# Batch 0 of an attention and gated FFN kernel, by blocks of 128 queries for all heads

## The chip, the core and the metric

The kernel runs on one core of a Trainium2 chip. The metric is the device time of one execution in microseconds (us); lower is better. A core has five engines that run side by side, each through its own queue in order: TensorE (PE in the profile, its weight loads PEld), VectorE (DVE), ScalarE (ACT), GpSimd (POOL) and SyncE (SP). They wait for each other by semaphores. Matrix products go into PSUM, a small memory that TensorE writes and ScalarE and VectorE read; all other tiles lie in SBUF.

## The reference

Eight batches of 576 queries and keys, eight heads of 64 columns, 16 extra "beacon" keys that every query sees:

```python
k_all = np.concatenate([beacon_k, k], axis=2)          # (8, 8, 16 + 576, 64)
v_all = np.concatenate([beacon_v, v], axis=2)
scores = q @ k_all.T / 8                               # causal on the 576, beacons always seen
a = softmax(scores)
x = (a @ v_all).transpose(0, 2, 1, 3).reshape(4608, 512)
g = x @ w_gate                                         # 512 -> 1536
out = (g * sigmoid(g) * (x @ w_val)) @ w_out           # 1536 -> 512
```

Inputs and output are float32; the kernel multiplies in bfloat16.

## The kernel before

**Data.** Queries and keys of batches 0 to 2 are loaded with 64 x 9 rows a head: partition p holds rows 9p to 9p + 8 (or, of a part of them, a shorter run). TensorE turns them (`turn`, tile `t_ps`) so that head columns lie on partitions, and VectorE or ScalarE copies them to `qT` and `kT` (`turned_copy`). Later batches are turned by DMA. GpSimd issues nearly all loads, since its transfers convert float32 to bfloat16 on the way; they go through one queue in order (`order_of_loads`). Only the first keys and queries of batch 0 (256 rows of heads 0 to 3, tile `first`) come by SyncE's and ScalarE's queues in float32, and are converted by VectorE and ScalarE (`regroup`, `regroup_second`); so are the beacon keys of batch 0 (`first_beacons`, converted by `cast_beacons`).

**Attention.** Two heads make a pair; a batch has four. Scores are made transposed (keys on partitions, queries along the row) in units. A unit is up to 512 columns of one pair, filled by a few matmuls into one tile `s_ps` (`scores`); ScalarE turns it into `p` by one exponential (`exponent`). `UNITS` lists the units of a pair: "A" has the first 240 queries (`HEAD`), "B", "C" and "D" the other 336 in wide pieces. The causal triangle is cut either on TensorE (a masked unit adds `below`) or afterwards by VectorE with `upper` or by GpSimd (`mask`). Value products take `p` as stationary operand (`pv`, tile `pv_ps`), one column more giving the sum of weights; `normalize` divides and writes `x`, tokens on partitions. Of batch 0, queries 0 to 239 go ahead: `pv_front`, `normalize_front`, `x_turn_front` and `x_copy_front` make the first 240 columns of `xT`, so that six gate tiles of 240 tokens can run before the rest is there; `x_turn` and `x_copy` then bring columns 240 to 575, a pair at a time.

**FFN.** `xT` is cut into nine chunks of 512 tokens. A gate tile (`ffn`, `gate_value`, tile `gv_ps`) makes 128 of the 1536 gate columns and the same value columns for one chunk, in two halves (G and H). ScalarE makes a tanh of the gate half (`tanh`), VectorE two products (`act1`, `act2`, tile `hT`). `project` multiplies by `wo`, `evacuate` copies and stores. In chunk 0 gate columns f = 0 to 5 come in two tiles each: 240 tokens (`HEAD`), then 272.

**Order.** PSUM has four slots; each of `t_ps`, `s_ps`, `pv_ps`, `gv_ps` and so on takes one (`take`), and it comes back when its last reader is done (`give`), first come, first served. The order of all work is written out by hand in the string `plan`: each letter is one piece (S and s scores, plain and masked; E exponential; D and M mask; P and p value products; Z, N, J, I the front's value products, normalizing, turn and copy; G, H gate halves; a, 1, 2 tanh and the two products; T turn; K, k, Q, q copies of turned keys and queries by VectorE and ScalarE; l a load; h a warming matmul pair; F a projection step). An engine runs its pieces in the order of the string. `warm` and `keep_warm` issue matmuls whose results nobody reads.

Of the kernel before, what the change touches and what calls it, by code (L numbers as in the profile page):

```python
# [33 lines left out]
FRONT = 4  # L34
# [35 lines left out]
FIRST_UNITS = "A0 A1 A2 A3 B0 C0 D0 B1 C1 D1 B2 C2 D2 B3 C3 D3"  # L70


HEAD = 240


def p_col(t, q):
    if t == 0:
        return q if q < HEAD else 368 + q - HEAD
    if t == 1:
        return 240 + q - 112 if q < HEAD else 784 + q - HEAD  # L80
    if t == 3:
        return 1120 + q - 368 if q < 496 else 1584 + q - 496
    return 1248 + q - HEAD if t == 2 else 704 + q - 496


@with_exitstack
def kernel(
# [88 lines left out]
    def keep_warm(ps):  # L176

        while heat:
            heat.pop()
            for row in range(2):  # L180
                r = slice(HALF * row, HALF * row + HALF)
                nc.tensor.matmul(ps[:, row, 0:P], lhsT=ident[r, :], rhs=ident[r, :], start=True, stop=True)  # L182
# [9 lines left out]
    first_beacons = static.tile([NB, H * D], FP32, name="first_beacons")  # L192
# [7 lines left out]
    p_first = static.tile([P, 2, 368], BF16, name="p_first")  # L200
# [73 lines left out]
    def cast_beacons():  # L274
        nc.vector.tensor_copy(beacons[0][0:NB, :], first_beacons[:])

# [9 lines left out]
    def turn(n):  # L286
# [3 lines left out]
        key = ("t", n)  # L290
        t_ps = turned[n] = take(key, [P, 2, 1024], BF16, "t_ps")
        parts[n] = 2 * len(pairs)
        side = sides.pop(n - NFT, None)
        for j, m in enumerate(pairs):
            by_head = qk[b % 2][:, 2 * RUN * m : 2 * RUN * (m + 1)].rearrange("p (h i d) -> p h i d", i=ROWS, h=2)
            for i in range(w):
                cols = slice(HALF * (w * j + i), HALF * (w * j + i + 1))
                for hh in range(2) if side is None else (None,):
                    for row in range(2):
# [3 lines left out]
                        halves(key, row, row, t_ps[o, row, cols], of, ident[r, r], 1, 1, True)  # L303
        if n >= NFT and 0 in pairs:
            beacon_turn(b, key, t_ps)
# [4 lines left out]
    def beacon_turn(b, key, t_ps):  # L310
# [14 lines left out]

    def first_beacon_turn():
        key = ("t", "beacons")
        t_ps = turned["beacons"] = take(key, [P, 2, 1024], BF16, "t_ps")
        beacon_turn(0, key, t_ps)

    def first_beacon_copy(eng):
        beacon_copy(0, turned["beacons"], eng)
        give(("t", "beacons"))

    def turned_copy(c, is_k, eng):
# [36 lines left out]
    def p_of(b, m, first):  # L372
        return p_first if b == 0 and m == NPAIR - 1 and first else pt[(NPAIR * b + m) % NPT]
# [32 lines left out]
    def exponent(n):  # L406
# [3 lines left out]
        nc.scalar.activation(p_of(b, m, u == "A")[:, :, c0 : c0 + w], ps[:, :, 0:w], ACT.Exp, scale=0.125)  # L410
# [21 lines left out]
    def pv_front(n):  # L432

        o_ps = fronts[n] = take(("z", n), [P, 2, 512], FP32, "pvf_ps")
        keep_warm(o_ps)
        for m in (2 * n, 2 * n + 1):
            for hh in range(2):
                for c in range(2):
                    for t in range(c + 1):
                        col = p_col(t, QBLOCKS[c][0])  # L440
                        at = 136 * (m % 2) + 68 * c
                        nc.tensor.matmul(
                            o_ps[:, hh, at : at + D + 1],
                            lhsT=p_of(0, m, True)[:, hh, col : col + P],
# [435 lines left out]
```

## Time and profile before

| | |
|---|---|
| median of 3 runs | 366.99 us (365.69 to 368.39) |
| the profiled execution | 366.46 us |
| its span, first to last instruction | 364.6 us |
| mean granted TensorE clock | 0.993 |
| TensorE busy | 353.5 us, 97% of the span |
| VectorE, ScalarE, GpSimd busy | 224.8, 186.0, 123.2 us |
| moved by DMA | 39.88 MB |

The durations come from one profiled execution. A row of a timeline gives start, length, engine, line, operation, output and inputs, how many instructions are merged, and in brackets how long the engine had been idle and what released it. A matmul's end is modelled, so its length holds some time in which the next already runs.

### The profile page before, as it was taken

Reading aid. Unit: us, or ns where it says so; the run is one execution under the profiler, and the core shown is the slowest. Engines: PE = TensorE matmul, PEld = TensorE weight load, DVE = VectorE, ACT = ScalarE, POOL = GpSimd, SP = SyncE. Lnnn points to the kernel's source line nnn. Section 1 sums busy time; section 2 is a strip of 40 time slices with the busy share of each in tenths; the row PEclk is TensorE's granted clock in tenths of the full one; section 3 lists DMA queues with packets and bytes.
Section 4 is the critical chain, followed back from the end, with each engine's and each line's share of the span. In section 5 each row is a group of like instructions: output and inputs, shape, how many; then the busy total and the mean of one; then the engine's idle time right before and its main releaser. Section 6 shows DMA issues by size and latency. Waiting matters only on the chain.

```text
span 364.6 us, 11957 instructions
## 1 busy us (share of the span) xinstructions
PE 353.5 (97%) x5202; PEld 200.8 (55%) x5202; DVE 224.8 (62%) x433; ACT 186.0 (51%) x280; POOL 123.2 (34%) x186
## 2 busy tenths in 40 slices
PE   5899999999999999999999999999999999999994
PEld 3678565654444565554565566546655554455543
DVE  5858986567766664487428753775567765364451
ACT  2875899822424777544863576457633323222310
POOL 8935677836237545365433013012000000000000
PEclk9899999999999999999999999999999999999999
DMA  9999999999999999999989829621413000110113
GB/s 150 155 199 194 189 192 135 179 133 181 178 131 111 135 134 126 150 178 137 120 138 139 106 39 112 105 15 21 110 59 67 0 2 3 58 59 2 59 59 117
DMA packets 146133, 39.88 MB, mean 109 GB/s; under 512 B 131488, under 2 KB 141728, under 8 KB 146080
## 3 DMA queue, kind: packets, MB, share of 16 engines
q0 software_dynamic: 97136, 18.87, 70.2%
q1 hardware_dynamic: 48512, 19.92, 28.9%
q8 instruction: 41, 0.67, 0.8%
q10 hardware_dynamic: 432, 0.33, 0.3%
q14 instruction: 12, 0.10, 0.1%
HBM read 38.27 MB, written 9.44 MB: 131 GB/s over the span
## 4 chain that ended last, share of the span: by engine, by line
PE 92%; ACT 4%; DMA 1%; DVE 1%; SPq 0%; issue 0%; DVEq 0%
PE gv_ps L168 51%; PE o_ps L168 25%; PE s_ps L168 6%; PE pv_ps L168 4%; PE pv_ps L498 4%; ACT p L410 3%; DMA first<-in_k_dram 1%; PE t_ps L166 1%; ACT kT L256 0%; PE xt_ps L541 0%; DVE hT L596 0%; DVE u L589 0%; SPq L661 0%; PE s_ps L182 0%; SPq L654 0%
## 5 line engine op out<-in xcount | busy, mean ns | idle before, releaser
L168 PE MATMUL gv_ps<-xT,wv 64*128 64x512 bf16 (+2 forms) x912 | 203.5, 365 | 0.0
L168 PE MATMUL gv_ps<-xT,wg 64*128 64x512 bf16 (+2 forms) x912 | 203.1, 365 | 0.1
L584 ACT ACTIVATE th<-gv_ps 128x512 f32<-128x512 f32 (+2 forms) x114 | 65.4, 575 | 117.9 <-PE gv_ps L168 117.6
L410 ACT ACTIVATE p<-s_ps 128x832 bf16<-128x832 f32 (+2 forms) x127 | 104.5, 873 | 32.6 <-PE s_ps L168 29.3
L168 PE MATMUL o_ps<-wo,hT 64*128 64x512 bf16 (+2 forms) x912 | 116.8, 365 | 0.2
L589 DVE SCALAR_TENSOR_TENSOR u<-th,gv_ps 128x512 f32<-128x512 f32 (+2 forms) x114 | 74.7, 656 | 65.1 <-ACT th L584 64.5
L168 PEld LDWEIGHTS <-wg 64*128 64x128 bf16 x912 | 82.3, 94 | 46.1 <-PE gv_ps L168 2.7
L168 PEld LDWEIGHTS <-wv 64*128 64x128 bf16 x912 | 81.6, 94 | 39.8 <-issue 0.7
L596 DVE SCALAR_TENSOR_TENSOR hT<-gv_ps,u 128x512 bf16<-128x512 f32 (+2 forms) x114 | 74.6, 661 | 3.0
L168 PEld LDWEIGHTS <-hT 64*128 64x128 bf16 x912 | 42.6, 94 | 33.5 <-PE o_ps L168 1.2
L219 POOL DMA_DIRECT2D vb<-in_v_dram x40 | 33.9, 850 | 66.5 <-PE s_ps L168 28.9
L168 PE MATMUL s_ps<-qT,kT 64*128 64x336 bf16 (+3 forms) x512 | 42.6, 253 | 1.6 <-ACT p L410 1.0
L168 PEld LDWEIGHTS <-kT 64*128 64x128 bf16 x512 | 24.2, 95 | 21.7 <-issue 1.1
L219 POOL DMA_DIRECT2D qk<-in_q_dram x25 | 21.3, 852 | 24.1 <-DMA qT<-qk 6.3
L527 DVE TENSOR_TENSOR x<-pv_ps,rec 128x640 bf16<-128x640 f32 (+1 forms) x32 | 25.3, 791 | 1.2
L419 DVE TENSOR_TENSOR p<-p,upper 128x256 bf16<-128x256 bf16 (+2 forms) x70 | 19.8, 308 | 9.5 <-ACT p L410 9.3
L526 DVE RECIPROCAL rec<-pv_ps 128x10 f32<-128x10 f32 (+1 forms) x32 | 6.8, 213 | 29.2 <-PE pv_ps L168 22.9
L219 POOL DMA_DIRECT2D qk<-in_k_dram x25 | 21.3, 855 | 8.2 <-PE gv_ps L168 4.7
L258 DVE COPY o_sb<-o_ps 128x512 f32<-128x512 f32 (+2 forms) x20 | 12.6, 653 | 18.1 <-PE o_ps L168 15.1
L423 POOL TENSOR_SCALAR_AFFINE_SELECT p<-p 128x256 bf16<-128x256 bf16 (+2 forms) x47 | 18.1, 404 | 14.9 <-ACT p L410 14.5
L168 PEld LDWEIGHTS <-p 64*128 64x128 bf16 x960 | 18.8, 94 | 4.5 <-PE pv_ps L168 0.2
L168 PE MATMUL pv_ps<-vb,p 64*128 64x65 bf16 x960 | 19.9, 189 | 0.0
(67 smaller groups left out, 144.6 us busy)
## 6 DMA issues: line engine op xcount, KB each, us to landing
out_dram<-o_sb SPq DMA_DIRECT2D x34, 256.0 KB, 2.7
vb<-in_v_dram POOLq DMA_DIRECT2D x24, 128.0 KB, 5.7
qk<-in_q_dram POOLq DMA_DIRECT2D x21, 128.0 KB, 5.3
qk<-in_k_dram POOLq DMA_DIRECT2D x16, 128.0 KB, 5.0
wo<-in_moe_w_out_dram POOLq DMA_DIRECT2D x2, 768.0 KB, 13.2
wg<-in_moe_w_gate_dram POOLq DMA_DIRECT2D x3, 384.0 KB, 10.9
wv<-in_moe_w_val_dram POOLq DMA_DIRECT2D x3, 384.0 KB, 12.6
qk<-in_k_dram POOLq DMA_DIRECT2D x2, 576.0 KB, 10.0
```

What stands on the lines that cost most here:

```text
L168: ins = nc.tensor.matmul(o, lhsT=l, rhs=r, start=start, stop=stop)
L219: return nc.gpsimd.dma_start(dst[p0 : p0 + n, c, :, 0:D], src[b, :, r : r + n, :].rearrange("h j d -> j h d"))
L258: eng.tensor_copy(o, i)
L410: nc.scalar.activation(p_of(b, m, u == "A")[:, :, c0 : c0 + w], ps[:, :, 0:w], ACT.Exp, scale=0.125)
L419: nc.vector.tensor_tensor(out=ap, in0=ap, in1=upper[:, None, d : d + w].to_broadcast([P, 2, w]), op=ALU.mult)
L423: nc.gpsimd.affine_select(out=ap, in_=ap, compare_op=ALU.is_ge, fill=0.0, base=d, pattern=[[0, 2], [1, w]], channel_multiplier=-1,)
L498: ins = nc.tensor.matmul(o_ps[:, side, 68 * c : 68 * c + D + 1], lhsT=pt[n % NPT][:, side, col : col + P], rhs=vb[b % 2][:, t, 2 * m + sid ...
L526: nc.vector.reciprocal(rec[:, :, c0:NKT], o[:, :, :, D : D + 1])
L527: nc.vector.tensor_tensor(out=xs[b][:, c0:NKT, P * m : P * m + P].rearrange("p c (h d) -> p h c d", d=D), in0=o[:, :, :, 0:D], in1=rec[:, ...
L584: nc.scalar.activation(th[:, 0:w], gvs[n][:, 0, 0:w], ACT.Tanh, scale=0.5)
L589: nc.vector.scalar_tensor_tensor(out=u[:, 0:w], in0=ths[n][:, 0:w], scalar=1.0, in1=gvs[n][:, 0, 0:w], op0=ALU.add, op1=ALU.mult)
L596: nc.vector.scalar_tensor_tensor(out=hTs[j][:, f, c0:c1], in0=gvs.pop(n)[:, 1, 0 : c1 - c0], scalar=0.5, in1=ths.pop(n)[:, 0 : c1 - c0], o ...
```

## The change

Batch 0 no longer goes in a front of 240 queries and a rest by pairs. It goes by query blocks: the first 240 queries, then 128, 128 and 80, and in each block all four pairs are done before the next. The parts:

- The turns of batch 0 are cut at 256 and at 384 rows (`FRONT`, `MIDDLE`), and so are its loads: K0m and Q0m bring rows 256 to 383 of all heads, K0t and Q0t the rest.
- Pairs 0 and 1 get a PSUM slot each for keys and for queries (`APART`) in their first turn. The beacon keys are turned into the slot of the first keys.
- The beacon keys of batch 0 are loaded by GpSimd as its first transfer, already converted; SyncE's transfer and VectorE's `cast_beacons` go.
- Score units "2", "3", "4" replace "B", "C", "D" in batch 0. Their matmuls are 128 or 80 columns wide, 112 matmuls instead of 64, with the same sum of columns.
- `pv_front` to `x_copy_front` now serve all blocks, so `pv`, `normalize`, `x_turn` and `x_copy` of batch 0 go.
- `p` of the fourth pair lies in a borrowed `hT` buffer (`lent`), since four pairs are open at a time.
- Chunk 0's gate tiles for f = 0 to 5: three of 240 tokens, three of 128, three of 368 and six of 144, fifteen instead of twelve.
- The plan is a new one up to the start of batch 1, and loads stand in a new order up to those of batch 2. The rest of the plan is the same.

The core of the diff:

```diff
-TURNS = [
-    (0, (0,), 0, FRONT), (0, (1,), 0, FRONT), (0, (2, 3), 0, FRONT), (0, (0, 1), FRONT, ROWS), (0, (2, 3), FRONT, ROWS)
-]
+FRONT, MIDDLE = 4, 6
+TURNS = [(0, (0,), 0, FRONT), (0, (1,), 0, FRONT), (0, (2, 3), 0, FRONT)]
+TURNS += [(0, m, i0, i1) for i0, i1 in ((FRONT, MIDDLE), (MIDDLE, ROWS)) for m in ((0, 1), (2, 3))]
+APART = 2
...
-FIRST_UNITS = "A0 A1 A2 A3 B0 C0 D0 B1 C1 D1 B2 C2 D2 B3 C3 D3"
-HEAD = 240
+UNITS["2"] = (368, 384, [(t, 128 * t, 240, 128) for t in range(3)], [(256, P, 0)])
+UNITS["3"] = (752, 512, [(t, 128 * t, 368, 128) for t in range(4)], [(384, P, 0)])
+UNITS["4"] = (1264, 400, [(t, 80 * t, 496, 80) for t in range(5)], [(320, 80, 0)])
+HEAD, BODY = 240, 368
...
-    p_first = static.tile([P, 2, 368], BF16, name="p_first")
+    lent = hT_pool.tile([P, NF, TOK], BF16, name="hT", tag="hT")
+    p_lent = lent[:].rearrange("p f t -> p (f t)")[:, 0 : 2 * P_W].rearrange("p (h w) -> p h w", h=2)
...
-        key = ("t", n)
-        t_ps = turned[n] = take(key, [P, 2, 1024], BF16, "t_ps")
-        parts[n] = 2 * len(pairs)
+        keys = [("t", n, 0), ("t", n, n < APART)]
+        for key in keys[: 1 + (n < APART)]:
+            turned[key] = take(key, [P, 2, 1024], BF16, "t_ps")
+            parts[key] = len(pairs) if n < APART else 2 * len(pairs)
+        parts[keys[0]] += n == 0
...
         if n < 16:
-            u, m = FIRST_UNITS.split()[n]
-            return 0, int(m), u
+            return 0, n % 4, "A234"[n // 4]
...
-    def x_turn_front(n):
-        if n == 0:
-            fronts["x"] = take("xf", [P, 2, 1024], BF16, "xf_ps")
+    def x_turn_front(n):
+        key = "xf" if n < 2 else ("xf", n)
+        if n != 1:
+            fronts[key] = take(key, [P, 2, 1024], BF16, "xf_ps")
...
-    ffn = [(0, f, c0, c1) for c0, c1 in ((0, HEAD), (HEAD, TOK)) for f in range(NF // 2)]
+    ffn = [(0, f, c0, c1) for c0, c1 in ((0, HEAD), (HEAD, BODY)) for f in range(NF // 4)]
+    ffn += [(0, f, 0, BODY) for f in range(NF // 4, NF // 2)] + [(0, f, BODY, TOK) for f in range(NF // 2)]
...
-    nc.sync.dma_start(
-        first_beacons[:].rearrange("j (h d) -> j h d", d=D), beacon_k[0].rearrange("h j d -> j h d")
-    )
...
     nc.scalar.activation(pt[1][:, 0, 0:1], pt[2][:, 0, 0:1], ACT.Exp)
+    beacon_load(0)
     runs(0, k, 4, H, 0, FRONT)
     runs(0, q, 4, H, 0, FRONT)
...
-    warm(8, TOK)
-    warm(4, P)
+    warm(7, TOK)
+    warm(6, P)
...
-    K0.0 Q0.0 v0.2 v0.1 v0.0 Q0.4 K0.4 v0.3 v0.4 v0.5 g0 u0 u1 g1 g2 u2 b1 K1 Q1 u3 g3 v1.2 v1.4 u4 g4 v1.0 K2 b2
+    K0m Q0m v0.2 v0.1 v0.0 K0t Q0t g0 u0 g1 u1 v0.3 v0.4 g2 u2 v0.5 b1 Q1 b2 K1 u3 g3 u4 v1.0 g4 Q2 K2 v1.3 v1.4
...
-    lb0h9ThlWQlAKhUTThllhqKlQhSlBsETKKQlEsSEEDQSlkZSlEDNEZsDlEJisTlhNEsDQhEJKhsllsslEEPIlElpSPsREllE
+    h0hTlWq9lTlhkAlSlTEhhlhlhBhhhqlqKKSElUlThsTsEEKKQDSllDsEElZlQSEZNJThNklqISDJlITlEsDGQKsEHSEDESa1
...
```

What this does to the engines' queues shows at three places. First GpSimd, from the fourth of its loads on; `upper` and `below` are the masks, `vb` values, `wg` and `wv` gate and value weights. Before:

```order
L209 DMA qk_101<-in_q_dram 64x4x320
L219 DMA vb_103<-in_v_dram 128x8x64
L685 AFFINE_SELECT upper<-upper 128x144
L219 DMA vb_103<-in_v_dram 112x8x64
L219 DMA vb_103<-in_beacon_v_dram 16x8x64
L209 DMA qk_101<-in_q_dram 64x4x320
L209 DMA qk_101<-in_k_dram 64x4x320
L679 AFFINE_SELECT below<-below 64x256 x2
```

After the change, from the same value load on:

```order
L226 DMA vb_102<-in_v_dram 128x8x64
L226 DMA vb_102<-in_v_dram 112x8x64
L226 DMA vb_102<-in_beacon_v_dram 16x8x64
L216 DMA qk_100<-in_k_dram 64x8x192
L216 DMA qk_100<-in_q_dram 64x8x192
L696 AFFINE_SELECT below<-below 64x256 x2
L255 DMA wg<-in_moe_w_gate_dram 128x4x128
L255 DMA wv<-in_moe_w_val_dram 128x4x128
L702 AFFINE_SELECT upper<-upper 128x144
```

`upper` moved from behind the first value load to behind the first two weight loads, and it now follows `below`.

Second ScalarE at its start, from its conversion of the first rows on (`p_109` to `p_111`, later `p_108` to `p_110`, are the three `p` buffers). Before:

```order
L256 ACTIVATE qk_101<-first 128x256
L256 ACTIVATE qT_105<-t_ps 128x256
L410 ACTIVATE p_109<-s_ps 128x2x368
L410 ACTIVATE p_110<-s_ps 128x2x368
L410 ACTIVATE p_111<-s_ps 128x2x368
L410 ACTIVATE p_first<-s_ps 128x736
L256 ACTIVATE kT_107<-t_ps 128x320
```

After:

```order
L263 ACTIVATE qk_100<-first 128x256
L263 ACTIVATE qT_104<-t_ps 128x256
L263 ACTIVATE kT_106<-t_ps 128x256
L418 ACTIVATE p_108<-s_ps 128x2x368
L263 ACTIVATE qT_104<-t_ps 128x256
L263 ACTIVATE qT_104<-t_ps 128x2x256
L418 ACTIVATE p_109<-s_ps 128x2x368
L418 ACTIVATE p_110<-s_ps 128x2x368
L418 ACTIVATE hT<-s_ps 128x2x368
```

Three more copies of turned rows are ScalarE's, two of them between the first exponential and the second.

Third ScalarE again, around the first tanh (`th`). Before:

```order
L410 ACTIVATE p_109<-s_ps 128x2x416
L410 ACTIVATE p_109<-s_ps 128x2x464
L584 ACTIVATE th<-gv_ps 128x240
L410 ACTIVATE p_109<-s_ps 128x2x416
L584 ACTIVATE th<-gv_ps 128x240
L256 ACTIVATE xT<-xt_ps 128x336 x2
```

After:

```order
L418 ACTIVATE p_110<-s_ps 128x2x512
L603 ACTIVATE th<-gv_ps 128x240
L418 ACTIVATE hT<-s_ps 128x2x512
L603 ACTIVATE th<-gv_ps 128x240
L418 ACTIVATE p_108<-s_ps 128x2x400
L418 ACTIVATE p_109<-s_ps 128x2x400
L263 ACTIVATE xT<-xf_ps 128x4x128
L603 ACTIVATE th<-gv_ps 128x240
L418 ACTIVATE p_110<-s_ps 128x2x400
L603 ACTIVATE th<-gv_ps 128x128
```

Before, one exponential of batch 0 was left at the first tanh; now five are, and tanh and exponentials alternate.

More of the change, by code (lines that the diff above doesn't have):

```diff
@@ L181, in keep_warm @@
                 r = slice(HALF * row, HALF * row + HALF)
-                nc.tensor.matmul(ps[:, row, 0:P], lhsT=ident[r, :], rhs=ident[r, :], start=True, stop=True)
+                nc.tensor.matmul(ps[:, row, at : at + P], lhsT=ident[r, :], rhs=ident[r, :], start=True, stop=True)
     ident = static.tile([P, P], BF16, name="ident")
@@ L302, in turn, with beacon_turn @@
                         of = side[r, i] if hh is None else by_head[r, hh, i0 + i]
-                        halves(key, row, row, t_ps[o, row, cols], of, ident[r, r], 1, 1, True)
+                        halves(keys[row], row, row, turned[keys[row]][o, row, cols], of, ident[r, r], 1, 1, True)
         if n >= NFT and 0 in pairs:
-            beacon_turn(b, key, t_ps)
+            beacon_turn(b, keys[0])
     BEACONS_AT = S
     parts = {}
-    def beacon_turn(b, key, t_ps):
+    def beacon_turn(b, key):
+        t_ps = turned[key]
         for mm in range(NPAIR):
@@ L324, in beacon_copy, with copied @@
         )
+    def copied(key, k):
+        parts[key] -= k
+        if not parts[key]:
+            give(key)
     def first_beacon_turn():
-        key = ("t", "beacons")
-        t_ps = turned["beacons"] = take(key, [P, 2, 1024], BF16, "t_ps")
-        beacon_turn(0, key, t_ps)
+        beacon_turn(0, ("t", 0, 0))
     def first_beacon_copy(eng):
-        beacon_copy(0, turned["beacons"], eng)
-        give(("t", "beacons"))
+        beacon_copy(0, turned["t", 0, 0], eng)
+        copied(("t", 0, 0), 1)
     def turned_copy(c, is_k, eng):
@@ L367, in unit, with p_of @@
         if n < 16:
-            u, m = FIRST_UNITS.split()[n]
-            return 0, int(m), u
+            return 0, n % 4, "A234"[n // 4]
         return n // 16, n % 16 // 4, "ABCD"[n % 4]
-    def p_of(b, m, first):
-        return p_first if b == 0 and m == NPAIR - 1 and first else pt[(NPAIR * b + m) % NPT]
+    def p_of(b, m):
+        return p_lent if b == 0 and m == NPAIR - 1 else pt[(NPAIR * b + m) % NPT]
     def scores(n, masked):
@@ L495, in pv @@
             for c, (q0, _) in enumerate(QBLOCKS):
-                for t in range(c + 1) if b or c > 1 else ():
+                for t in range(c + 1):
                     col = p_col(t, q0)
@@ L533, in normalize @@
         give(("p", n))
-    xts = {}
-    def x_turn(m):
-        t_ps = xts[m] = take(("x", m), [P, 2, 1024], BF16, "xt_ps")
-        for c, (q0, n) in enumerate(QBLOCKS):
-            if q0 >= HEAD:
-                nc.tensor.transpose(t_ps[:, 0, q0 : q0 + n], xs[0][0:n, c, P * m : P * m + P], ident[0:n, 0:n])
-    def x_copy(m, eng):
-        copy(eng, xT[:, m, HEAD:S], xts.pop(m)[:, 0, HEAD:S])
-        give(("x", m))
     def x_transpose(b):
@@ L837 @@
+    FaHFaFF1FFF12FHa2FG1GFHF2HFaF1FoaFFoFFFFFG2FF1FFHFaF1FGFF2HGFFFaFF12FH2FFaFFFFF1FFFFF2oFFFFFFFFF
+    FFFOFFFFFFOFFFFOFFFOFFFFOFFFFFFFFOo
     """
```

179 lines of the change are left out of this document (94 added, 85 removed).

## The prediction

> **What bounds the kernel now.** I read the page first, then busy time by stretch, then the timelines of the first 37 us, and last the chain that ended last.
>
> ```profile
> PE 353.5 (97%) x5202; PEld 200.8 (55%) x5202; DVE 224.8 (62%) x433; ACT 186.0 (51%) x280; POOL 123.2 (34%) x186
> ```
>
> TensorE is busy for 97% of the span, so only about 11 us are open at all. The view by stretch says where they lie (columns: busy us of PE, PEld, DVE, ACT, POOL with instruction counts, then PE's granted clock, DMA share, GB/s):
>
> ```profile
> 0.00:4.82 4.82, 3.29 (x8) 1.16 (x9) 2.64 (x16) 1.91 (x3) 3.62 (x10) 1.00 0.58 123
> 4.82:8.22 3.40, 1.19 (x49) 0.78 (x51) 1.58 (x4) 0.00 (x0) 3.40 (x7) 1.00 1.47 187
> 8.22:11.64 3.42, 3.42 (x132) 2.96 (x120) 2.73 (x8) 1.84 (x3) 3.35 (x6) 0.51 1.75 167
> 11.64:15.05 3.41, 2.69 (x48) 1.90 (x45) 2.91 (x12) 3.40 (x6) 3.41 (x5) 0.99 1.96 142
> 21.45:26.93 5.48, 5.42 (x117) 4.38 (x115) 3.48 (x10) 3.71 (x8) 1.77 (x3) 1.00 1.26 204
> 26.93:37.03 10.10, 9.88 (x193) 8.03 (x192) 8.24 (x21) 5.87 (x16) 5.44 (x7) 1.00 1.49 197
> 72.00:364.60 292.60, 287.62 (x3888) 155.00 (x3884) 172.50 (x306) 132.35 (x196) 70.95 (x107) 1.00 0.87 94
> ```
>
> Behind 21.45 TensorE hardly stops, and the change rewrites only batch 0 and the first gate tiles. So its worth is decided in the first 37 us: TensorE stands still for 2.2 us between 4.82 and 8.22, and then runs a stretch of 3.4 us at half clock. From 11.64 on ScalarE has no gap (3.40 of 3.41), and TensorE waits for its exponentials. The chain starts like this (start, us, what):
>
> ```profile
> 1.61 0.83 SPq L661
> 2.50 4.95 DMA first<-in_k_dram
> 7.55 0.44 DVE qk L258
> 8.03 0.71 PE t_ps L166 x48
> ```
>
> The beacon keys' transfer (L661) stands on SyncE ahead of the second pair's keys, and these open the first transposes. My yardstick is the first gate tile that is 512 wide (f = 6). It starts at 37.03 before; in both kernels batch 0, half the first chunk and a little of batch 1 lie ahead of it. Before the change 18 transposes fewer and two score units more are done there, 0.25 us each way, so the two starts can be compared.
>
> ```profile
> 6.77 0.32 PE L166 MATMUL t_ps<-ident,qk 64*64 64x64 bf16 x16 [1.49 <-DVE qk L258]
> 9.29 0.82 PE L168 MATMUL s_ps<-qT,kT 64*128 64x240 bf16 x8
> 12.49 0.52 PE L442 MATMUL pvf_ps<-vb,p 128*128 128x65 bf16 x12
> 21.45 0.27 PE L168 MATMUL gv_ps<-xT,wg 64*128 64x240 bf16 x1
> 37.03 0.38 PE L168 MATMUL gv_ps<-xT,wg 64*128 64x512 bf16 x1
> ```
>
> These are before's milestones: first transposes, first scores, first value products, first gate tile, yardstick. I work out the same five for the changed kernel, following each engine's queue and each PSUM slot.
>
> **1. The start, beacon keys and keys of pair 1.**
>
> ```profile
> 5.81 0.71 DVE L275 CAST beacons<-first_beacons 16x512 bf16<-16x512 f32 x1 [1.72 <-DMA first_beacons<-in_beacon_k_dram]
> 7.55 0.43 DVE L258 CAST qk<-first 128x512 bf16<-128x512 f32 x1 [0.83 <-DMA first<-in_k_dram]
> 4.35 0.42 ACT L256 ACTIVATE qk<-first 128x256 bf16<-128x256 f32 x1 [0.63 <-DMA first<-in_k_dram]
> ```
>
> The first keys are there at 4.35, when ScalarE casts its half. VectorE's half stood behind the beacon cast until 6.45; that cast goes, so both halves are done at 4.77, and the transposes start when the warming matmuls end, at about 5.1 instead of 6.77. The keys of pair 1 move from SyncE's third place to its second, from 2.50 to 1.61. Their transit lies between that of the first keys (0.81 to 4.35, 3.5 us) and the 4.95 us of the chain: landing at 5.1 to 6.6, taken as 5.9. Cast, turn 1, beacon copy and six warming matmuls follow: first scores at **6.85, 2.4 us earlier**. The beacon keys, first on GpSimd, need at most the same 4.2 us as on SyncE (1.61 to 5.81) from 1.33, so 5.5; they are wanted at 6.3.
>
> **2. ScalarE up to the fourth exponential.**
>
> ```profile
> 8.40 0.39 ACT L256 ACTIVATE qT<-t_ps 128x256 bf16<-128x256 bf16 x1 [3.63 <-PE t_ps L166]
> 11.65 0.78 ACT L410 ACTIVATE p<-s_ps 128x736 bf16<-128x736 f32 x1 [0.35 <-PE s_ps L168]
> 12.33 0.78 ACT L410 ACTIVATE p_first<-s_ps 128x736 bf16<-128x736 f32 x1
> 13.31 2.48 ACT L410 ACTIVATE p<-s_ps 128x832 bf16<-128x832 f32 x3
> 15.63 0.63 ACT L256 ACTIVATE xT<-xf_ps 128x480 bf16<-128x480 bf16 x1
> ```
>
> Two exponentials of 736 columns start 0.68 apart though each shows 0.78: back to back they overlap by 0.1. Exponential 0 runs 7.4 to 8.15. Then two copies of queries, now ScalarE's, hold it until 9.0 (0.39 and about 0.64, less the overlap), and scores 1 come behind 14 warming matmuls. Exponentials 1 to 3 end at 11.4, against 13.11 (12.33 + 0.78): **1.7 us earlier**, 0.7 of the lead being spent.
>
> **3. GpSimd, the mask and the first gate tile.**
>
> ```profile
> 5.16 0.37 POOL L685 TENSOR_SCALAR_AFFINE_SELECT upper<-upper 128x144 bf16<-128x144 bf16 x1
> 8.12 0.90 POOL L679 TENSOR_SCALAR_AFFINE_SELECT below<-below 64x256 bf16<-64x256 bf16 x2
> 12.22 1.50 POOL L248 DMA_DIRECT2D wv<-in_moe_w_val_dram  x2
> 11.84 0.47 DVE L419 TENSOR_TENSOR p<-p,upper 128x224 bf16<-128x224 bf16 x2
> ```
>
> The triangle `upper`, ready at 5.53 before, is now built behind ten transfers, `below` and two weight loads. Transfers at 0.6 to 0.95 us each, the selects at 0.90 and 0.37: `below` is ready at 9.55, `upper` at **11.4**. Masks 0 and 1 wait for it and end at 12.37, and the first value products start at 12.42 against 12.49: the rest of the lead is gone here, and nothing queued behind the masks on VectorE (one copy of queries, the normalizing) gets out sooner. From there normalizing, turning and copying x run at once instead of behind other work: first gate tile at **16.05 instead of 21.45**. Its weights landed by 16.3 before; 336 KB of values now stand behind them, so about 14. The batch's remaining keys and queries come in shorter runs (256 and 384 bytes written instead of 640), for which this trace has no row; even 2 us more is covered.
>
> **4. Gate tiles among exponentials.** What a tile costs VectorE and ScalarE, by width:
>
> ```profile
> L589 DVE SCALAR_TENSOR_TENSOR u<-th,gv_ps 128x512 f32<-128x512 f32 x5 | 3.4, 681 | 0.1
> L589 DVE SCALAR_TENSOR_TENSOR u<-th,gv_ps 128x272 f32<-128x272 f32 x6 | 2.6, 434 | 0.8 <-ACT th L584 0.8
> L589 DVE SCALAR_TENSOR_TENSOR u<-th,gv_ps 128x240 f32<-128x240 f32 x6 | 2.4, 399 | 1.5 <-ACT th L584 1.5
> 16.08 6.47 ACT L410 ACTIVATE p<-s_ps 128x832 bf16<-128x832 f32 x8
> 23.03 0.86 ACT L410 ACTIVATE p<-s_ps 128x832 bf16<-128x832 f32 x1
> 22.73 0.37 ACT L584 ACTIVATE th<-gv_ps 128x240 f32<-128x240 f32 x1 [0.18 <-PE gv_ps L168]
> ```
>
> Tile 0 fills its slot at 16.05, but its tanh stands behind exponentials 8 to 10 and starts at 19.0, and its second product gives the slot back at 20.5. With four slots, TensorE then waits for exponentials 9 (18.15), 10 (19.1) and 11 (20.3): about 0.5 us each time. From 15.5 on ScalarE has nine exponentials (0.7 to 0.95 each, 7.35), five tanh (1.3) and two x copies (1.1), 9.75 us. It also waits for TensorE and slots, which wait for VectorE's products; following these hops I get 2.0 us of gaps: exponential 15 ends at **27.25, against 23.89**. This is 3.4 us later, but tiles 0 to 5 and part of 6 are then done, where before only one or two were.
>
> **5. The rest.** Behind 27.25 TensorE has the last value products (40 at 0.03, 1.2 us), three tiles 368 wide (1.23 each, 0.6 done, 3.05), six 144 wide (0.48 each, 2.9), and transposes and one score unit (0.9): 8.0 us. At 144 columns, however, the rows above extrapolate to about 0.3 for each of two products, 0.55 a tile, longer than TensorE's 0.48; a tile's slot comes back late, which I make 1.4 us of waits. The yardstick starts at 27.25 + 8.0 + 1.4 = 36.65, against 37.03: **0.4 us earlier**. 96 more matmuls (gate and score columns being the same in sum) cost 0 to 0.5, taken as 0.
>
> **The clock.** Before, the clock is halved behind a stretch with 1.19 of 3.40 busy and full behind one with 2.69. In my timeline 4.82 to 8.22 has about 2.2 busy, nearer to the second, so I count full clock. If it falls, two score units and the warming matmuls of 8.2 to 11.6 take 0.6 longer in front of ScalarE. The Trainium skill (TensorE: Matmul & The Clock Gate, "HAM oscillation — how this bites in real kernels") says that it takes a gap of over some 3.4 us to lose the clock. By that rule the term would be nothing; the trace disagrees, since the longest gap ahead of its fall is 1.49 us.
>
> **The far side.** Loads of later batches stand in other order, with the same bytes ahead of the output weights.
>
> ```profile
> L252 POOL DMA_DIRECT2D wo<-in_moe_w_out_dram x1: 826/826/826, 42.2 to 42.2; - x1
> DMA to landing us min/median/max: 14.3/14.3/14.3
> 58.40 0.81 PE L168 MATMUL o_ps<-wo,hT 64*128 64x512 bf16 x6
> ```
>
> Their second half lands at 42.2 + 14.3 = 56.5 and is first wanted at 58.40, so a gain over about 1.9 us would meet that transfer.
>
> **Rivals.** *Holes closed (0.20).* If the slots come back in time, ScalarE closes its 2.0 us of gaps and VectorE's 1.4 vanish: 3.8 us earlier at the yardstick, of which the output weights leave about 1.9. For it: ScalarE had no gap from 11.64 on. Against: a tanh in its queue now delays slots. 365.1 us.
>
> *Ping-pong (0.25), slower.* Place: a gate tile's slot between tanh and second product, 16 to 36 us. If each hop takes the full duration instead of overlapping by 0.1 (ScalarE) or 0.08 (VectorE), the same chain gives 27.9 for exponential 15 and 38.1 for the yardstick, 1.1 late: 368.1 us. It decides from the point where exponential 15 ends after 27.6. For it: the 240-wide tiles before waited 1.5 us for tanh. A quarter of this case passes 370.7, where waits are doubled again.
>
> *No head start (0.10).* If the keys of pair 1 land at 7.4 as before, because three queues now fetch at once, exponentials 1 to 5 come 0.8 later: 367.4 us.
>
> **How the numbers follow.** The profiled execution took 366.46 us, 1.86 around its span of 364.6; the median of the runs is 366.99, 0.53 higher. 366.46 - 0.4 = 366.1, on the scale of the median **366.6** (0.45). About 1% (3.7 us) is what a measurement of this kernel tells from no change. My own case spreads by 1 us, the rivals from 365.1 to 368.1 and beyond, and single runs by 2.7 us: 363.7 to 369.5 holds 8 in 10. Faster by over 1% needs all 3.8 us and no clip: 0.06. Slower: the quarter of ping-pong and little else, 0.08. Within 1%: 0.86.
>
> **What would show it.** In the changed profile: first transposes near 5.1, scores near 6.9; VectorE's first mask waiting for `upper` until 11.4; first gate tile near 16; TensorE's waits no longer for VectorE's cast but for exponentials and products between 17 and 36; last exponential of batch 0 near 27. I am wrong if the first gate tile comes after 18, if the clock falls again after 12, or if the 512-wide tile starts outside 35 to 38.5.

## The result, and the profile after

The changed kernel takes **370.36 us** (median of 4 runs, 368.50 to 372.25) against 366.86 for the kernel before in the same runs: ratio 1.0117, 95% interval 1.008 to 1.0154. It is slower by 1.2%, where I had forecast no change. Measured again later it gives 370.47 against 365.94, ratio 1.0125, interval 1.0071 to 1.018. The profiled execution took 369.59 us with a span of 367.6, so 3.0 us more span than before.

These stretches can be set beside those of before (same columns; the last one, not shown there, had a clock of 1.00):

```profile
4.82:8.22 3.40, 2.33 (x83) 1.69 (x82) 0.95 (x3) 1.44 (x4) 3.40 (x5) 1.00 1.51 164
8.22:11.64 3.42, 2.49 (x82) 1.88 (x82) 1.78 (x4) 2.94 (x6) 3.30 (x7) 1.00 1.82 154
11.64:15.05 3.41, 3.32 (x73) 2.50 (x69) 2.90 (x11) 2.42 (x4) 3.41 (x6) 0.66 1.46 148
15.05:18.46 3.41, 3.41 (x100) 2.75 (x93) 2.48 (x8) 3.08 (x5) 3.30 (x5) 0.84 1.61 163
```

and the five milestones, with the mask that they hang on, so (timelines of TensorE and VectorE):

```profile
5.27 0.43 PE L173 MATMUL t_ps<-ident,qk 64*64 64x64 bf16 x16
7.11 0.32 PE L175 MATMUL s_ps<-qT,kT 64*128 64x240 bf16 x4
11.72 0.86 DVE L427 TENSOR_TENSOR p<-p,upper 128x224 bf16<-128x224 bf16 x4 [0.41 <-POOL upper L702]
12.13 0.55 PE L455 MATMUL pvf_ps<-vb,p 128*128 128x65 bf16 x8
16.75 0.26 PE L175 MATMUL gv_ps<-xT,wg 64*128 64x240 bf16 x1
40.02 0.38 PE L175 MATMUL gv_ps<-xT,wv 64*128 64x512 bf16 x1
```

The start is early as forecast, and the first gate tile is 4.7 us ahead of before. The yardstick, however, comes at 40.02 instead of 37.03. TensorE's longest waits after the first gate tile lie here:

```profile
26.65 0.40 PE L496 MATMUL xf_ps<-ident,x 128*128 128x128 bf16 x4 [1.19 <-DVE hT L615]
39.04 0.23 PE L175 MATMUL gv_ps<-xT,wg 64*128 64x144 bf16 x1 [1.01 <-issue]
60.74 0.44 PE L529 MATMUL pv_ps<-vb,p 128*128 128x65 bf16 x9 [0.71 <-issue]
```

"<-issue" means that nothing the profile records was waited for. I numbered TensorE's records in order of start, weight loads and semaphore waits included. The first instructions behind these three gaps have, to within one record, the numbers 962, 1474 and 2242, and each of these is 194 more than a multiple of 256. That pointed to a line of the page that I had passed over (queue, packets, MB, share; before has the same line):

```profile
q8 instruction: 41, 0.67, 0.8%
```

41 packets for about 10,400 instructions before and 10,600 now are some 256 instructions each. One of them was moved shortly ahead of each gap's end, in the midst of full queues. This is the DMA view from 23.9 to 25.2 us: the first line has busy tenths of the 16 engines in 40 slices, then the packets, and the two queues in use.

```profile
DMA  9999999999999999999999999999999989999999
...
DMA packets 412, 0.27 MB, mean 204 GB/s; under 512 B 214, under 2 KB 411, under 8 KB 411
...
q0 software_dynamic: 411, 0.25, 132.4%
q8 instruction: 1, 0.02, 4.6%
```

By the packets' own times, that transfer ran from 24.11 to 25.07, 3.9 us after TensorE had executed number 706 (20.18), and number 962 started 1.6 us after its end. The next ones repeat this: a boundary at 32.89, a transfer from 36.46 to 37.36, the next boundary at 39.04. So the **theory**: TensorE's instructions come in blocks of 256, and a block is asked for about when TensorE enters the one ahead of it. With full queues, lag (3.2 to 3.9 us), transfer (about 1.0) and start-up (1.3 to 1.7) make some 6.2 us a block, whatever the instructions are.

How long does TensorE need for a block? A pair of gate matmuls (two row halves, with two weight loads four instructions) follows the last after 63 ns at 144 columns, 103 at 240, 116 at 272 and 216 at 512 (medians of the starts in both traces). 64 pairs are 4.0, 6.6, 7.4 and 13.8 us. Tiles 240 wide and more take longer than the 6.2 us and hide the fetch; the changed kernel's 144-wide tiles don't, and its score matmuls, cut to 128 and 80 columns, bring more instructions in the same way.

The rivals were the chain of slots and exponentials (my slower rival), the half clock between 12.7 and 16.2 us, and the late mask.

### The profile page after: what moved, and what is told of

Same layout as the page of the kernel before. It is cut to its first block, busy times and chain, and to the rows that moved or that the text cites. A ratio compares the mean times of both kernels' runs of the same rounds, so it can differ in the third digit from the quotient of the medians.

```text
span 367.6 us, 12165 instructions
## 1 busy us (share of the span) xinstructions
PE 355.6 (97%) x5301; PEld 203.0 (55%) x5301; DVE 224.8 (61%) x437; ACT 187.9 (51%) x284; POOL 126.1 (34%) x188
## 4 chain that ended last, share of the span: by engine, by line
PE 91%; ACT 4%; DVE 2%; DMA 1%; issue 1%; SPq 0%; DVEq 0%
PE gv_ps L175 50%; PE o_ps L175 25%; PE s_ps L175 6%; PE pv_ps L175 4%; PE pv_ps L529 2%; ACT p L418 2%; PE pvf_ps L455 1%; DMA first<-in_k_dram 1%; PE t_ps L173 1%; ACT hT L418 1%; DVE p L427 1%; PE xf_ps L496 0%; ACT th L603 0%; ACT qT L263 0%; DVE hT L615 0%
## 5 line engine op out<-in xcount | busy, mean ns | idle before, releaser
L175 PE MATMUL gv_ps<-xT,wg 64*128 64x512 bf16 (+4 forms) x936 | 204.9, 360 | 1.9 <-issue 1.0
L175 PE MATMUL gv_ps<-xT,wv 64*128 64x512 bf16 (+4 forms) x936 | 205.3, 360 | 0.0
L603 ACT ACTIVATE th<-gv_ps 128x512 f32<-128x512 f32 (+4 forms) x117 | 66.0, 565 | 117.6 <-PE gv_ps L175 117.0
L418 ACT ACTIVATE p<-s_ps 128x736 bf16<-128x736 f32 (+4 forms) x124 | 102.5, 864 | 33.5 <-PE s_ps L175 29.8
L608 DVE SCALAR_TENSOR_TENSOR u<-th,gv_ps 128x512 f32<-128x512 f32 (+4 forms) x117 | 75.2, 644 | 72.0 <-ACT th L603 71.2
L615 DVE SCALAR_TENSOR_TENSOR hT<-gv_ps,u 128x512 bf16<-128x512 f32 (+4 forms) x117 | 75.2, 648 | 3.1
L175 PEld LDWEIGHTS <-kT 64*128 64x128 bf16 x560 | 25.3, 95 | 22.2 <-issue 1.6
L427 DVE TENSOR_TENSOR p<-p,upper 128x256 bf16<-128x256 bf16 (+2 forms) x71 | 21.4, 331 | 7.9 <-ACT p L418 7.3
L557 DVE TENSOR_TENSOR x<-pv_ps,rec 128x640 bf16<-128x640 f32 x28 | 23.1, 825 | 1.1
L556 DVE RECIPROCAL rec<-pv_ps 128x10 f32<-128x10 f32 x28 | 6.1, 217 | 28.5 <-PE pv_ps L175 23.0
L265 DVE COPY o_sb<-o_ps 128x512 f32<-128x512 f32 (+2 forms) x20 | 12.7, 654 | 17.6 <-PE o_ps L175 14.5
```

The lines of the kernel that those rows point to most:

```text
L175: ins = nc.tensor.matmul(o, lhsT=l, rhs=r, start=start, stop=stop)
L265: eng.tensor_copy(o, i)
L418: nc.scalar.activation(p_of(b, m)[:, :, c0 : c0 + w], ps[:, :, 0:w], ACT.Exp, scale=0.125)
L427: nc.vector.tensor_tensor(out=ap, in0=ap, in1=upper[:, None, d : d + w].to_broadcast([P, 2, w]), op=ALU.mult)
L556: nc.vector.reciprocal(rec[:], o[:, :, :, D : D + 1])
L557: nc.vector.tensor_tensor(out=xs[b][:, :, P * m : P * m + P].rearrange("p c (h d) -> p h c d", d=D), in0=o[:, :, :, 0:D], in1=rec[:].to_br ...
```

## Experiments

**1. The same columns in more instructions, in the kernel before.** Two kernels cut the matmuls of six gate tiles in two. Each has 192 instructions more on TensorE; one has them at 32 to 42 us and the other at 263 to 276.

```
+ cuts = ((c0, 368), (368, c1)) if j == 0 and c0 == HEAD else ((c0, c1),)   # first
+ cuts = ((0, 256), (256, TOK)) if j == 6 and f < 6 else ((c0, c1),)         # second
+ for a, z in cuts:
```

> The kernel before, with every matmul of the six gate tiles 272 wide cut into two, 128 and 144 columns wide: the same columns, slots, activations, products, loads and order, and 96 more matmuls, each with its weight load, so 192 more instructions on TensorE; nearly all lie ahead of the yardstick (first gate tile 512 wide, 37.03 before). Theory 1, instruction fetch: in the trace of the changed kernel TensorE stands still for 1.18 us at 26.64 and for 1.01 us at 39.04, and both times the next instruction is the 194th behind a multiple of 256 (962 and 1474); the instruction queue's transfer of 16,384 bytes ended 1.6 us ahead of it. If TensorE's instructions come in blocks of 256 that need 6.1 to 6.4 us each while the DMA queues are full, then 192 more of them are 4 to 5 us of fetch, of which before has some 2 us to spare: stalls at indices 962, 1218, 1474 or 1730, the yardstick at 38.5 to 40, and 1.5 to 3 us slower as a whole. Theory 2, slots and ScalarE (my slower rival): nothing of this chain changes; 96 weight loads lie beside matmuls, the yardstick within 0.5 of 37.03, and the time within 0.7 us of before.

> The same edit as in the first split, at another place: in the kernel before, the matmuls of six gate tiles of the seventh chunk, each 512 wide, are cut into two of 256 columns: again 96 more matmuls with their weight loads, 192 instructions, the same columns, slots and products, but at some 250 us, where a block of 256 instructions takes TensorE about 13 us and the DMA queues are nearly empty (the instruction transfers there start within 1 us of the block's end). Theory 1 (fetch while the queues are full): no stall, within 0.5 us of before. Rival (96 matmuls and weight loads more cost TensorE their time wherever they stand): 3.8 us slower, as the first split was. Nothing is left out of the computation.

The first: 370.38 us against 366.57, ratio 1.0106 (1.0087 to 1.0126), with no other edit. The second: 365.20 against 366.51, ratio 0.9966 (0.9938 to 0.9994). The trace of the first has four waits that before's first profile lacks, at the numbers 706, 962, 1218 and 1474 (timelines of TensorE's matmuls):

```profile
22.14 0.51 PE L498 MATMUL pv_ps<-vb,p 128*128 128x65 bf16 x11 [1.10 <-issue]
29.13 0.26 PE L168 MATMUL gv_ps<-xT,wv 64*128 64x240 bf16 x1 [0.69 <-issue]
35.32 0.21 PE L168 MATMUL gv_ps<-xT,wg 64*128 64x128 bf16 x1 [0.95 <-DVE hT L598]
41.37 0.18 PE L168 MATMUL s_ps<-ident,below 64*128 64x16 bf16 x2 [2.06 <-issue]
```

Their sum is 4.8 us, and the yardstick comes at 42.13. Not all of it is the split's: its first added instruction is number 1058, at 31.84, so the waits at 706 and 962 (1.8 us) stand ahead of it, where the two kernels have the same instructions. There this execution, the slowest of six, fetched more slowly than before's first profile (the block's transfer started 3.86 us behind number 450, against 2.69), and before's second profile waits 0.47 us at 706 as well. At number 1058 it is 1.95 us behind before's first profile. The other 3.15 us up to the yardstick come behind that, and there the waits at 1218 and 1474 are 3.0 us.

Slots, activations and order were untouched, so the ping-pong can't be the reason. Nor can 96 weight loads as such: the late ones cost nothing. That case is not quite the same, since its pieces are 256 wide, 109 ns a pair and 7.0 us a block, longer than a fetch. That short blocks can pass where they are brought sooner is seen in the changed kernel's trace: it runs the block from number 4546 (147.26) in 4.20 us without a wait, and the transfer of the next started 0.54 us behind that boundary. That the late instructions even gained 1.3 us was not expected; experiment 5 is about it.

**2. The changed kernel with room in the queues.** Seven transfers are issued some 10 us later.

```
- FREE_LOADS = 24
+ FREE_LOADS = 20     # and 7 loads of the plan moved to just ahead of the first gate tile 512 wide
```

> The changed kernel with seven of its transfers (the last parts of the gate and value weights, keys and queries of batch 2 and values of batch 1) issued some 10 us later, so that the DMA queues run empty at about 31 us, ahead of the block of TensorE's instructions that is run from 39.04. Theory 1: that block's transfer, which started 3.6 us after the block boundary at 32.89, starts within about 1.5 us of it, and the stall of 1.01 us at index 1474 is gone, while the one at 962 (26.64), where the queues are still full, stays at 1 us or more. Rival (the transfer's lag is a fixed time of TensorE's prefetch and has nothing to do with other transfers): lag 3.6 us again and the stall stays. The time as a whole is no test: the weights come later, so TensorE may wait for them; 370 to 376 us.

The total says nothing (376.70 us; TensorE waits 5.97 us for gate weights at 46.58, as the loads come late). The blocks say it: in the full stretch the lags are 3.52 and 3.83 us, with waits at 706 and 962.

```profile
21.80 0.21 PE L175 MATMUL s_ps<-ident,below 64*128 64x64 bf16 x4 [0.59 <-issue]
28.27 0.34 PE L496 MATMUL xf_ps<-ident,x 128*128 128x128 bf16 x3 [1.35 <-DVE hT L615]
```

Then the queues empty. The next transfer starts 1.09 us behind its boundary, and the one after it, alone in the DMA view from 33.5 to 35.2, starts at 33.82, even 0.7 us before TensorE executes number 1218:

```profile
DMA  0000000900000000000000000000000000000000
...
DMA packets 1, 0.02 MB, mean 10 GB/s; under 512 B 0, under 2 KB 0, under 8 KB 0
...
q8 instruction: 1, 0.02, 3.9%
```

Number 1474 starts at 39.42 without a wait, 4.91 us behind 1218. The lag thus depends on the other transfers, and the rival of a fixed lag falls.

**3. The changed kernel with fewer instructions, and with more.** The first cuts the first chunk into 12 gate tiles, 96 instructions fewer with the same columns; the second adds 24 warming instructions at 11.5 us.

```
+ ffn = [(0, f, 0, HEAD) for f in range(NF // 4)] + [(0, f, 0, BODY) for f in range(NF // 4, NF // 2)]
+ ffn += [(0, f, HEAD if f < NF // 4 else BODY, TOK) for f in range(NF // 2)]   # 12 tiles
```

> The changed kernel with its first chunk of gate work cut into 12 tiles instead of 15: three of 240 columns early, three of 368, and then three of 272 and three of 144 for the rest (those that were 144 and 128 wide become one piece where both are due at once); the same columns in sum, 96 fewer TensorE instructions. Theory 1 (fetch): 96 instructions are 0.37 of a block, 2.3 us at 6.1 to 6.4 us a block, so that at least one of the stalls at 26.64 and 39.04 shrinks: yardstick at 38 to 39 against 40.02, and 1 to 2.3 us faster than the changed kernel. Theory 2 (slots): the 144-wide tiles with their long activations and products become fewer, so this also speeds up TensorE by at most the waits of those tiles, which in the trace of the changed kernel sum to less than 0.4 us: 0 to 0.4 us faster, with the stalls of over 1 us still at 26.6 and 39.0.

> The changed kernel with six more pairs of warming matmuls ahead of the scores of the fifth unit, 24 more instructions on TensorE at about 11.5 us, where TensorE waits for VectorE and a clock of 0.50 follows at 12.75. Theory 1 (fetch): the two stalls stay at the same instruction numbers, 962 and 1474, so that they move to other work, 24 instructions earlier in the program, at 26.6 and 39.0 or a few tenths earlier; the yardstick does not get earlier than 39.8 whether or not the clock falls, since the lead is taken back by the fetch: total within 0.5 us of the changed kernel. Theory 3 (half clock between 12.6 and 16.2 is what is missing): the clock stays at 1.00, the first gate tile starts at about 16.1 instead of 16.75 and the yardstick 0.6 us earlier at 39.4, total 0.6 us faster. If the clock falls anyway, this tells only of the stalls.

With 12 tiles the yardstick is at 38.56, as the fetch theory said; the wait at 962 is 0.58 and the one at 1474 is gone. But the time is 370.58 us: no gain, and there my expectation was wrong. The trace shows two places where the lead is given back:

```profile
61.75 0.32 PE L175 MATMUL s_ps<-qT,kT 64*128 64x336 bf16 x2 [1.26 <-DVE x L557]
...
153.04 0.09 PEld L175 LDWEIGHTS <-wv 64*128 64x128 bf16 x1 [1.38 <-issue]
```

The first is a slot that VectorE gives back later than TensorE now wants it. The second, seen in the weight loads (its matmuls stand still for 0.89 us), is number 4802, which is 194 more than a multiple of 256 again. TensorE ran the block ahead of it in 5.41 us, and the transfer had started 3.02 us behind the boundary. The changed kernel passes its number 4802 without a wait, and faster, but with the lag of 0.54 us named above; why the lags differ there is open. No other trace has a wait of over 0.35 us at a boundary behind 75 us.

With 24 instructions more, the waits stay at the numbers 962 and 1474 (1.91 and 0.76 us; one of 0.66 at 706 is new), and that puts the first in front of other work: a gate tile's matmul instead of the transposes of x.

```profile
27.53 0.23 PE L175 MATMUL gv_ps<-xT,wg 64*128 64x128 bf16 x1 [1.91 <-issue]
```

So the "DVE hT" named at 26.65 in the changed kernel's trace was not what ended that wait. The program says the same: these transposes need x, and a slot, from one normalizing of VectorE, which was done 2.0 us earlier.

```profile
23.98 0.69 DVE L479 TENSOR_TENSOR x<-pvf_ps,rec 128x512 bf16<-128x512 f32 x1
```

The clock fell all the same (0.70 and 0.80 in the two stretches from 8.22), so this run doesn't test the clock. 371.19 us, ratio 1.0132 (1.0110 to 1.0154).

**4. The late mask, and the changed kernel again.**

```
+ plan: U (select of upper) behind the second load; before, behind ten      # first
+ cuts = ((0, 256), (256, TOK)) if j == 6 and f < 2 else ((c0, c1),)        # third; the second is unchanged
```

> The changed kernel with the triangle `upper` selected by GpSimd behind its second transfer instead of behind ten, `below` and two weight loads: VectorE's first mask no longer waits until 11.7 but for its exponential (8.3 or so). Theory 1 (fetch): the first value products may start 0.5 to 1 us earlier than 12.13, but TensorE reaches the block boundaries 706 and 962 no earlier than the blocks, so the yardstick stays within 0.5 us of 40.0 and the time within 0.7 us of the changed kernel's 370.4. Rival (my third step: the late mask spends the lead): the yardstick 0.7 to 1 us earlier, 369.4 us.

> The changed kernel, unchanged, in the same call as the next two, for a second profile and for a narrower interval. The theory (a block of 256 TensorE instructions comes no faster than every 6.1 us while the DMA queues are full, and the next one is asked for only when TensorE enters the one before) expects stalls of over 0.5 us at the same indices, 962 and 1474, whatever the start of the program did in this run, and a last matmul 4 to 5.5 us later than in the kernel before (359.58 and 359.99); the time 370 to 371.5 us. If the stalls were chance, they are elsewhere.

> The changed kernel with the matmuls of two gate tiles of the seventh chunk, 512 wide, cut in two: 64 more instructions at some 250 us, where 192 cost nothing. By this the last block boundary (10690) comes to stand about 18 instructions ahead of the end of the program, as it does in the kernel before (10434 of 10446), where the transfer of one block more begins 1.8 us behind the boundary, in the middle of the last output transfers, whose last packets then end at 362.94 instead of 361.4 to 361.5. Theory of the tail: the same happens here, and the last output lands 1.3 to 1.6 us later: 371.7 us against 370.4. Rival (the tail of before has another reason): within 0.5 us of the changed kernel.

The early mask gave 372.66 us, ratio 1.0154 (1.0105 to 1.0203): not faster, but also not within the 0.7 us that I expected. In its profile no mask waits for `upper`, yet the second transposes start at 7.43, the clock is 0.50 to 0.54 from 8.22 to 18.46, and the first mask starts at 12.53, behind late copies of keys. The yardstick is at 43.52, with waits of 1.90 and 1.29 us at 962 and 1474. I can't separate these from the edit, so what the late mask costs is not shown. The repeated profile of the changed kernel has its waits at the same three numbers (1.17, 1.10 and 0.75 us), and TensorE's last matmul starts at 364.96 (364.31 the first time) against 359.58 and 359.99 in two profiles of before: 4.3 to 5.4 us later.

The third kernel, which is the changed one up to 270 us, answers the question of the clock by chance. Its clock never fell:

```profile
8.22:11.64 3.42, 3.11 (x87) 2.38 (x83) 1.12 (x3) 2.33 (x4) 3.30 (x7) 1.00 1.86 158
11.64:15.05 3.41, 3.03 (x64) 2.41 (x62) 1.93 (x8) 3.08 (x4) 3.41 (x5) 1.00 1.44 155
15.05:18.46 3.41, 3.30 (x94) 2.63 (x92) 2.87 (x10) 2.20 (x4) 2.45 (x4) 1.00 1.52 151
```

Yet its yardstick is at 42.17, later than with the half clock. The chain of blocks shows how the profiles part. Times at which TensorE executes each boundary, and the steps between them:

| profile | 450 | 706 | 962 | 1218 | 1474 | yardstick |
|---|---|---|---|---|---|---|
| before | 15.90 | +5.11 | +6.16 | +6.63 | +7.25 | 37.03 |
| changed | 14.66 | +5.52 | +6.47 | +6.25 | +6.14 | 40.02 |
| changed, again | 15.01 | +5.69 | +6.35 | +6.47 | +6.20 | 40.69 |
| changed, full clock | 16.56 | +6.05 | +6.47 | +6.25 | +5.87 | 42.17 |
| before, first split | 15.95 | +6.19 | +6.99 | +6.20 | +6.04 | 42.13 |

In the changed kernel the yardstick comes 25.4 to 25.7 us behind number 450 in all three profiles, whatever the clock did (27.2 us with the early mask, where a transfer's lag reached 4.2). Before needs longer than 6.6 us a block from 962 on by its own matmuls, so the fetch is hidden there. At 706 and 962 it has no time to spare: it passes them 1.4 us behind the end of the transfer. In the row of the first split, the steps to 706 and 962 lie ahead of the split.

**5. The end of the program.** TensorE's last matmul came 4.7 us later than before, but the span is only 3.0 longer. A second profile of before shows where the rest is.

> The kernel before, unchanged, for a second profile: in the first one 5.0 us lie between the start of TensorE's last matmul (359.58) and the end of the span, against 3.3 to 3.6 in the changed kernel and in the first four experiments, although the end of the program is the same. If that tail is chance, it is 3.3 here, and the kernel before has a span of about 363 with TensorE's work as it was; if it belongs to the kernel, it is 5.0 again. No stall of over 0.5 us at an index 194 behind a multiple of 256 (706, 962, 1218, 1474) is expected, since none was there.

The tail was 5.3 us again (359.99 to 365.3), so it belongs to the kernel. In before, boundary 10434 lies 12 instructions ahead of the end. The transfer of one block more starts 1.8 to 2.1 us behind it (361.28 in the first profile), in the midst of the last stores. The DMA view of before from 361.0 to 363.2, and its issues of 355 to 372:

```profile
DMA  7999999630000000000000000000000100000000
GB/s 233 298 270 261 252 540 270 187 84 9 0 0 0 0 0 0 0 0 0 0 0 0 9 9 9 9 9 9 9 9 9 9 19 19 19 0 0 0 0 0
...
q8 instruction: 1, 0.02, 2.7%
...
out_dram<-o_sb SPq DMA_DIRECT2D x1, 64.0 KB, 3.1
out_dram<-o_sb ACTq DMA_DIRECT2D x1, 64.0 KB, 3.3
```

The stores are all but done at 361.5; then one trickle of 512-byte packets is left, which goes on when the instruction packet is through (362.23), and ends at 362.94. Without a transfer in that place, as in the kernel with the late split, the same stores land so (DMA view from 359.5 to 363):

```profile
out_dram<-o_sb SPq DMA_DIRECT2D x1, 64.0 KB, 1.6
out_dram<-o_sb ACTq DMA_DIRECT2D x1, 64.0 KB, 1.7
```

From the last matmul's start to the last packet's end it is 3.36 and 3.60 us in the two profiles of before, 1.96 and 1.97 in those of the changed kernel, and 1.96 with the late split. The changed kernel has 198 instructions more, and its last boundary is far from the end. The 64 late instructions of the last kernel of experiment 4 put it back to 16 from the end, and the trickle returns:

```profile
q8 instruction: 1, 0.02, 2.3%
...
out_dram<-o_sb SPq DMA_DIRECT2D x1, 64.0 KB, 3.0
out_dram<-o_sb ACTq DMA_DIRECT2D x1, 64.0 KB, 3.2
```

From the last matmul to the last packet it is 3.31 us there. Of all 13 profiles, the three with an instruction transfer among the last stores have 3.3 to 3.6 us; the other ten have 1.95 to 1.97. The median of the last kernel is 372.22 against 370.47 for the changed kernel. The ratios to before, 1.0151 (1.0097 to 1.0206) and 1.0125 (1.0071 to 1.0180), overlap, so the trace shows this step and the time alone would not.

**6. One part alone, and the best of both.**

```
- first_beacons, its SyncE transfer and VectorE's cast
+ beacon_load(0) as GpSimd's first transfer        # and, in the second kernel, the late split
```

> One part of the change alone: the beacon keys by GpSimd's first transfer, converted on the way, so that VectorE's cast goes and the second pair's keys are second on SyncE; the order of the work by heads stays as before, and TensorE's instructions are as many as before. My step 1 says: first transposes at about 5.2 instead of 6.77 and first scores at about 7.1 instead of 9.29. Theory 1 (fetch): a head start of up to 2 us brings TensorE to the block boundaries earlier, but the blocks come no sooner than every 6.1 us, so that the start's gain is taken back at index 962 (27.18 before, transfer ended at 25.80) by a stall of 0.5 to 1.2 us: yardstick at 36 to 36.6, 0.4 to 1 us faster as a whole. Theory 2 (ScalarE and slots): the gain stays where ScalarE's exponentials start earlier: exponential 15 about 1.5 us earlier than 23.89, the yardstick at about 35.5, 1.5 us faster, if the output weights do not hold it.

> The kernel before with both edits that cost nothing where they stand: the beacon keys by GpSimd's first transfer (one part of the change), and 96 matmuls of the seventh chunk cut in two, which takes the last block boundary away from the end of the program. Theory: the second alone gave 1.3 us; the first alone gave 0.4 us in the median with the boundary still at the end; together 1.3 to 2 us faster than before, 364.6 to 365.2 us. Rival for the first (a head start at the beginning is worth nothing, since the blocks of instructions and the output weights set the pace): no better than 365.2.

The beacon part alone: 366.21 us against 366.57, ratio 0.9998 (0.9969 to 1.0027). Its second transposes came at 7.30 (8.03 before) and the clock stayed at 1.00, but number 450 was executed at 15.68 (15.90 before), number 962 at 26.83 (27.18) and the yardstick at 36.67 (37.03). The last matmul starts at 359.44 against 359.58: the head start is worth next to nothing, though I had expected 0.4 us or more. The fetch isn't what spent it: most of it was gone at number 450, whose block had landed at 12.09, and the wait of 0.5 to 1.2 us that I expected at 962 is not there. What spent it is open. This profile has its last boundary where before has it, but no transfer behind it, and why is open; its last packets end 1.96 us behind the last matmul's start, so it takes the transfer to delay them. Its 12 runs spread from 364.37 to 369.53. With the late split: 365.23 us against 365.94, ratio 0.9971 (0.9943 to 0.9999). It beats both kernels, but no more than the split alone (0.9966), so its gain can be the tail's alone.

## Why the prediction was wrong

I forecast 366.6 us and 363.7 to 369.5; it was 370.36.

- **Step 1 held.** First transposes 5.27 (5.1 forecast), first scores 7.11 (6.85). The second pair's keys vary, though: their transposes start at 6.58 to 7.43 in seven profiles with this start.
- **Step 2 held**: the fourth exponential (the timeline's row of ScalarE below) ends at 11.74; I had 11.4.

```profile
10.96 0.78 ACT L418 ACTIVATE hT<-s_ps 128x736 bf16<-128x736 f32 x1
```

- **Step 3 held** in its order: the mask waits for `upper` until 11.72 (11.4), first value products 12.13 (12.42). First gate tile 16.75 for 16.05.
- **The clock** didn't stay full: 0.66 and 0.84 between 11.64 and 18.46. I had priced that at 0.6, and the first gate tile is 0.7 late. But the yardstick did not hang on it, as the run at full clock shows. The rule that it takes a gap of some 3.4 us (the Trainium skill, TensorE: Matmul & The Clock Gate, "HAM oscillation — how this bites in real kernels") disagrees with this trace too: TensorE's longest gap between its first transposes (5.27) and the fall (12.75) was 0.66.
- **Step 4** was right up to 21 us: the waits for exponentials that I put at 0.5 each are 0.48, 0.33 and 0.22 (the last three of these rows of TensorE's timeline; the first row is the gap of 0.66 just named).

```profile
6.68 0.32 PE L173 MATMUL t_ps<-ident,qk 64*64 64x64 bf16 x16 [0.66 <-DVE qk L265]
...
18.94 0.26 PE L175 MATMUL gv_ps<-xT,wg 64*128 64x240 bf16 x1 [0.48 <-ACT p L418]
19.86 0.36 PE L175 MATMUL s_ps<-qT,kT 64*128 64x80 bf16 x10 [0.33 <-ACT p L418]
21.04 0.43 PE L455 MATMUL pvf_ps<-vb,p 128*128 128x65 bf16 x9 [0.22 <-ACT hT L418]
```

  Exponential 15 then ends at 28.90 (27.25). 1.19 of these 1.65 us are the wait at number 962, behind which the copy of x stands on ScalarE.
- **Step 5 is the one that failed**, in the term "96 more matmuls cost 0 to 0.5, taken as 0". It was right for the array: columns times time per column are 49.6 us in both kernels up to the same later place (66.08 us before, 70.74 now; 216 ns for a pair 512 wide are 0.42 ns a column). It left out that each is an instruction, with a weight load beside it, to be fetched. As many more matmuls of the same columns cost the kernel before 3.8 us (370.38 against 366.57). In the changed kernel the waits at 962 and 1474 are 2.2 us (1.19 + 1.01) of the 4.7 by which TensorE ends later. The third, 0.71 at 2242, can't simply be added: it is followed by a wait of 0.38 for VectorE's normalizing, and where number 2242 comes without a wait, as in the run at full clock, that one is longer:

```profile
65.36 0.32 PE L175 MATMUL s_ps<-qT,kT 64*128 64x336 bf16 x2 [1.27 <-DVE x L557]
```

  So 2.5 us I did not take apart by runs. Up to the same later place TensorE's idle time grew by 2.6 us in all and its busy time by 2.0 (62.04 against 60.01), and a modelled length can hold a short wait. The tail then gives 1.7 us back, which I had not forecast either; 4.7 - 1.7 is the 3.0 us of the span.
- **The rivals.** Ping-pong named the right sign and even the point (exponential 15 after 27.6), but not the mechanism: the first split slows before as much without touching a slot. A slot that came late did add a part, in the wait just shown. "No head start" was a small part of the scatter. The output weights landed at 56.8, as forecast, and held nothing.

## What to carry to other kernels

Count an engine's instructions as a load of their own: in a stretch with full DMA queues, compare the time of 256 instructions of the new code with the time in which a block arrives (6.2 us here), and prefer wider matmuls where the first is shorter. Waits that the profile gives to "issue", or to an engine long done, are worth numbering: if the numbers agree modulo 256, as here, look at the instruction transfers. Where the last boundary falls just ahead of the program's end, the block behind it can delay the last stores.

## What the hardware did that I had not expected

- An instruction transfer took about 1 us. In the changed kernel it started 3.2 to 3.9 us behind its boundary between 14 and 43 us, with full queues, and within 1 us, or earlier, at 21 of 28 boundaries behind 100 us, where they were quieter. The next block ran 1.3 us behind its end at the earliest, in all 13 profiles, and 1.3 to 1.7 us behind it where TensorE had to wait.
- The look-ahead was one block: in 13 profiles no block's transfer started more than 2.1 us before TensorE passed the boundary ahead of it. The Trainium skill (Runtime: NRT & Kernel Launch, "Instruction fetch mechanics") states blocks of 16 KiB or 256 instructions, which these traces agree with. It also calls the cost of crossing a block's boundary mostly hidden: that holds where the queues are quiet, and the waits of 0.5 to 2.1 us at boundaries show that it doesn't where they are full.
- 192 instructions more at 263 to 276 us made the kernel 1.3 us faster. The last boundary moved away from the end, and no instruction transfer fell among the last stores.
